# A local-attention and MLP kernel: a chunk's q, k and v fetched for all four head pairs by one set of transfers

## The chip, the cores and the metric

The kernel runs on one core of one Trainium2 chip. The time is the device time of one execution in microseconds (us), and runs are compared by their median. The names of the engines are those of the profile: PE is TensorE (matmuls), PEld its weight loads, DVE VectorE, ACT ScalarE, POOL GpSimd, SP SyncE, which here does nothing but issue DMA transfers. "SPq" is the queue of instructions on SP.

## The reference

There are 4 batches, 8 heads, 768 positions and a head dimension of 64. Attention sees the first `n_global` = 8 keys and, of the others, the last `n_local` = 96 positions up to the query, with a bias that falls linearly with the distance; its output goes through an MLP of width 512 to 2048 to 512.

```python
scores = matmul(q, k.T) / sqrt(64)
keep   = (pos_k < n_global) | ((rel >= 0) & (rel < n_local))       # rel = pos_q - pos_k
scores = where(keep, scores - slope[h] * dist, -1e9)
x      = softmax(scores) @ v                                       # heads side by side: (3072, 512)
out    = gelu(x @ w_in) @ w_out                                    # w_in 512 x 2048, w_out 2048 x 512
```

All values arrive in single precision except the weights, which arrive as 64-bit words and are decoded on the chip.

## The kernel before

**Chunks and pairs.** The 3072 positions are cut into 12 chunks of 256 (`CT`), three to a batch; `c` counts chunks, and a chunk with `c % 3 == 0` is the `first` of its batch and has fewer keys. The 8 heads go in 4 pairs (`p`), two heads of 64 on the 128 partitions. For each chunk and pair there is a sequence: `load` fetches q, k and v; `split` scales q on POOL (L167, one instruction for a pair); `scores_pair` (L312) makes the scores on PE and reduces them on DVE (L346); `exps` (L356) takes the exponentials on ACT (L363) and normalises on DVE for chunks 0 and 1, on POOL for the others (L372); `flip` transposes on PE (L382) and copies the result `pt` out of PSUM on ACT (L386); `av_pair` (L389) multiplies with v on PE (L412) and writes x as two parts, `xh` on ACT (L435) and the remainder `xl` on DVE (L436, which shows as the helper's line L173).

**The MLP.** The width 2048 is cut into 8 slices of 256 (`s`). `m1` (L449) makes a slice of the hidden layer from x, three products for each operand pair, since both sides are split in a high and a low part; `gelu` evaluates it twice on ACT (L459, L460) with the remainder on DVE; `m2` (L479) accumulates the output.

**The weights.** Each slice comes in 4 pieces of 512 KB (`load_words`, L178, names `w`). `split_weights` decodes a piece on ACT (L203) and DVE (L209, L211, L213), `part_weights` makes its high part on ACT (L223) and its low part on DVE. There are 4 buffers for pieces under way, so a later piece is issued only when an earlier one is decoded. Later the same words are fetched a second time and compared (`check_load`, `check_words`, names `c`).

**The order of work.** `run` walks through numbered steps T and emits, at each, what the tables say. `STEPS` holds the MLP's steps: chunks 0 and 1 go through the slices in turn, so that the weights are decoded while two chunks use them; from chunk 2 on, a chunk goes through its 8 slices alone. `DECODE` says at which step a piece is decoded. `START[c]` is the step from which chunk c's attention is counted, and `EVENTS[c]` gives for each of its operations the step (relative to that) of each pair: `EVF` for chunks 0 and 1, `EV2` for chunk 2, `EVS` for the rest. `after` adds an order between two instructions. Within what data and these orders require, a scheduler places the instructions of each engine; each engine then works strictly in its order, SP too.

**Loads.** Chunk 0 is fetched by `load_first` in whole-chunk buffers. For every other chunk `load(c, p)` issues the transfers of one pair, all on SP through the local helper `sync` (L279): 1 for q, 5 for k and 6 for v, 12 in all (8 in a first chunk), 48 for a chunk. Each pair has its own buffers out of a pool of four sets:

```python
self.nat = pool("nat", 4)
kr = pool.tile([P, KW + 96 if cc == 0 else 2 * KW], F32, name=f"kr{c}_{p}", tag="kn", padded_shape=[P, 2 * KW])
qr = pool.tile([P, CT], F32, name=f"qr{c}_{p}", tag="qn")
vr = pool.tile([P, 4, 2, 64], F32, name=f"vr{c}_{p}", tag="vn")
```

so that pair p of a chunk can be fetched when pair p of the chunk before has been used up. In `run`, chunk 1's four loads stand between the 4 pieces of the first weight slice and those of the others:

```python
for i in range(4):
    self.load_weights(0, i)
for p in range(NP):
    self.load(1, p)
for s in range(1, NST - 1):
    for i in range(4):
        self.load_weights(s, i)
```

Chunk 2's loads are ordered behind the last piece of the third slice, `word_ins[2, 3]`, and check pieces behind the loads of earlier steps.

Of the kernel before, what the change touches and what calls it, by code (L numbers as in the profile page):

```python
# [7 lines left out]
F32 = mybir.dt.float32  # L8
# [8 lines left out]
B, H, S, D = 4, 8, 768, 64  # L17
P = 128
# [15 lines left out]
MAXLOCAL = 97.0  # L34

START = [-7, -3, 7] + [8 * c - 7 for c in range(3, NCH)]
EVF = {"load": (-9, -9, -9, -9), "split": (-1, -1, -1, -1), "s": (0, 1, 2, 3), "pt": (2, 3, 4, 5), "av": (2, 3, 4, 5)}
EV2 = {"load": (-4, -3, -1, 1), "split": (-1, 1, 3, 5), "s": (0, 2, 4, 6), "pt": (1, 3, 5, 7), "av": (2, 4, 6, 8)}
EVS = {"load": (-4, -3, 0, 1), "split": (-2, -1, 2, 3), "s": (0, 0, 4, 4), "pt": (2, 3, 6, 7), "av": (4, 4, 8, 8)}
EVENTS = [EVF, EVF, EV2] + [EVS] * (NCH - 3)  # L40


# [40 lines left out]
class Fast:  # L83
    def __init__(self, tc, ctx, qT, kT, v, w, out, limits):
        self.tc, self.nc = tc, tc.nc
        self.qT, self.kT, self.v, self.w, self.out = qT, kT, v, w, out
        self.limits = limits
        pool = lambda name, bufs=1, **k: ctx.enter_context(tc.tile_pool(name=name, bufs=bufs, **k))
        self.ctx = ctx
        self.early = ExitStack()  # L90
        self.es = self.early.enter_context(tc.tile_pool(name="es", bufs=1, side="right"))
        self.const = pool("const")
        self.wts = pool("wts")
        self.stg = pool("stg", 3)
        self.nat = pool("nat", 4)
        self.pp = pool("pp", 6)
        self.ptp = pool("ptp", 2)
        self.xp = pool("xp", 3)
        self.gp = pool("gp", 2)
        self.sm = pool("sm", 2)  # L100
        self.words = ExitStack()
        self.ws = self.words.enter_context(tc.tile_pool(name="ws", bufs=4))
        self.ps_acc = pool("ps_acc", 2, space=PSUM)
        self.ps = pool("ps", 6, space=PSUM)
        self.win, self.wout = {}, {}
        self.kt, self.qt, self.vt, self.raw = {}, {}, {}, {}
# [134 lines left out]
    def load_first(self):  # L241

        nc = self.nc
        kr = self.es.tile([P, NP, KW + 96], F32, name="kr0")
        qr = self.es.tile([P, NP, CT], F32, name="qr0")
        vr = self.es.tile([P, 4, DM], F32, name="vr0")
        every = [[S, P], [P * S, NP]]
        nc.sync.dma_start(qr[:, 0], dap(self.qT, 0, [[S, P], [1, CT]]))
        nc.sync.dma_start(kr[:, 0, 0:CT], dap(self.kT, 0, [[S, P], [1, CT]]))
        nc.scalar.dma_start(qr[:, 1:NP], dap(self.qT, P * S, [[S, P], [P * S, NP - 1], [1, CT]]))  # L250
        nc.sync.dma_start(kr[:, :, CT:CT + 96], dap(self.kT, 0, every + [[1, 96]]))
        nc.sync.dma_start(kr[:, :, CT + 96:], dap(self.kT, 0, every + [[1, NG]]))
        nc.sync.dma_start(kr[:, 1:NP, 0:CT], dap(self.kT, P * S, [[S, P], [P * S, NP - 1], [1, CT]]))
        self.load_v(nc.scalar.dma_start, vr, 0, 0, DM)
        for p in range(NP):
            v = vr[:, :, p * P:(p + 1) * P].rearrange("q n (h d) -> q n h d", h=2)
            self.raw[0, p] = (kr[:, p], qr[:, p], v)

    def load_v(self, dma, vv, v0, cc, w):
        row = lambda r, n: dap(self.v, v0 + r * DM, [[DM, n], [1, w]])  # L260
        q0 = cc * CT
        if cc:
            dma(vv[0:NC, 0, :], row(q0 - 32, NC))
            dma(vv[NC:P, 0, :], row(0, NG))
        else:
            dma(vv[:, 0, :], row(0, P))
        dma(vv[0:NG, 1, :], row(0, NG))
        dma(vv[NG:P, 1, :], row(q0 + 96, NC))
        for j in range(2) if cc else (1,):
            o = HQ * j if cc else 0  # L270
            dma(vv[o:o + HQ, 2:4, :],
                dap(self.v, v0 + (q0 + j * P - 96) * DM, [[DM, HQ], [160 * DM, 2], [1, w]]))

    def load(self, c, p):
        nc = self.nc
        b, cc = divmod(c, CPB)

        def sync(out, in_):
            ins = nc.sync.dma_start(out, in_)  # L279
            if c == 2:  # L280
                self.after(ins.ins, self.word_ins[2, 3], "behind the first slices")
            return ins

        k0 = (b * H + 2 * p) * D * S
        v0 = b * S * DM + p * P
        pool = self.nat
        kr = pool.tile([P, KW + 96 if cc == 0 else 2 * KW], F32, name=f"kr{c}_{p}", tag="kn", padded_shape=[P, 2 * KW])
        qr = pool.tile([P, CT], F32, name=f"qr{c}_{p}", tag="qn")
        vr = pool.tile([P, 4, 2, 64], F32, name=f"vr{c}_{p}", tag="vn")
        self.last_load = sync(qr, dap(self.qT, k0 + cc * CT, [[S, P], [1, CT]])).ins  # L290
        if cc == 0:
            sync(kr[:, 0:CT], dap(self.kT, k0, [[S, P], [1, CT]]))
            sync(kr[:, CT:CT + 96], dap(self.kT, k0, [[S, P], [1, 96]]))
            sync(kr[:, CT + 96:], dap(self.kT, k0, [[S, P], [1, NG]]))
        else:
            q0 = k0 + cc * CT
            sync(pairs(kr, NG, 352, NX + NC), dap(self.kT, q0 - 96, [[S, P], [192, 2], [1, NX + NC]]))
            sync(kr[:, 224:288], dap(self.kT, q0 + HQ, [[S, P], [1, NX]]))
            sync(kr[:, KW:KW + NX], dap(self.kT, q0 + 32, [[S, P], [1, NX]]))
            for o in (0, 192):  # L300
                sync(pairs(kr, o, 352, NG), dap(self.kT, k0, [[S, P], [0, 2], [1, NG]]))
        self.load_v(sync, vr.rearrange("p n h d -> p n (h d)"), v0, cc, P)
        self.raw[c, p] = (kr, qr, vr)

    def split(self, c, p):
        kr, qr, vr = self.raw.pop((c, p))
        self.hi_pool(qr, qr, self.qsc[:, p:p + 1])
        self.kt[c, p], self.qt[c, p] = kr, qr
        for hh in range(2):
            self.vt[c, 2 * p + hh] = vr[:, :, hh, :]  # L310

    def scores_pair(self, c, p):  # L312

# [75 lines left out]
    def av_pair(self, c, p):  # L389
# [3 lines left out]
        if p == 0:  # L393
            self.x[c] = (self.xp.tile([P, NP, CT], F32R, name=f"xh{c}", tag="xh"),
                         self.xp.tile([P, NP, CT], F32R, name=f"xl{c}", tag="xl"))
        if EVENTS[c] is EVS:
            if p % 2 == 0:
                return
            ps = range(p - 1, p + 1)
        else:  # L400
            ps = range(p, p + 1)
# [3 lines left out]
            av = [avb[:, j] for j in range(2)]  # L405
        else:
            av = [self.bank([P, n, P], f"av{c}_{p}_{j}") for j in range(2)]
        heads = {(i, hh): (self.pt_t.pop((c, 2 * q + hh)), self.vt.pop((c, 2 * q + hh)))
                 for i, q in enumerate(ps) for hh in range(2)}

        def add(out, lhs, rhs, start, stop):
# [11 lines left out]
        for i in range(n):  # L423
            for a in range(2):
                for j in range(2):
                    if first and j == 0:
                        continue
                    ks = slice(0, HQ) if first else slice(j * HQ, (j + 1) * HQ)
                    for hh in range(2):
                        pt, vt = heads[i, hh]  # L430
                        qs = slice(a * HQ, (a + 1) * HQ)
                        add(av[j][hh * D:(hh + 1) * D, i, qs], vt[ks, 2 + a, :], pt[ks, 2, qs], False, True)
        for j in range(2):
            xh, xl = (x[:, ps.start:ps.stop, j * P:(j + 1) * P] for x in self.x[c])
            nc.scalar.copy(xh, av[j])  # L435
            self.lo_dve(xl, av[j], xh)  # L436
# [64 lines left out]

    def run(self, flag_i):
# [14 lines left out]
        for self.T in range(START[0] - 1, last):  # L517
# [234 lines left out]
```

## Time and profile before

| what | value |
|---|---|
| median of 3 runs | 723.93 us (720.51 to 725.51) |
| the profiled execution's own time | 724.53 us |
| its span, first to last instruction | 722.7 us |
| mean granted PE clock | 0.974 |
| PE busy | 682.6 us (94%), 5485 matmuls |
| ACT busy | 358.9 us (50%) |
| DVE busy | 285.4 us (39%) |
| POOL busy | 108.5 us (15%) |
| DMA | 71.29 MB in 87164 packets, 99 GB/s over the span |

The profile is of one execution. Its views group instructions by source line, list what each engine waited for and what released it, follow the chain of work that ended last back from the end, and show the instructions in order of time. An engine's idle time costs something only where the end hangs on it. A wait for several things is put down to the one that came last. In views, `out<-in` names the tiles that an instruction writes and reads, and an x with a number counts instructions in a row.

### The profile page before, as it was taken

To read this page: it belongs to the slowest core of one execution; us is meant where nothing else is said; L and a number is where in the kernel's file an instruction comes from. 1 tells how busy PE (TensorE), PEld (TensorE's weight loads), DVE (VectorE), ACT (ScalarE), POOL (GpSimd) and SP (SyncE) were. 2 spreads that over 40 slices of the span, in tenths; PEclk is the share of its full clock that TensorE was granted. 3 is DMA by queue.
4 is the path that set the end of the run, shared out by engine and by line. 5 is a ranking of instruction groups with operands and counts; after the bars stand their busy time and mean duration, and the time that the engine had idled before them with its cause. 6 is when DMAs were issued, how large, how long until landed. Compare 5 with 4: busy or idle time off the path is not lost.

```text
span 722.7 us, 14534 instructions
## 1 busy us (share of the span) xinstructions
PE 682.6 (94%) x5485; PEld 595.3 (82%) x5485; DVE 285.4 (39%) x987; ACT 358.9 (50%) x868; POOL 108.5 (15%) x232
## 2 busy tenths in 40 slices
PE   6757888999999999999999999999999999999996
PEld 4445767788888988998988988988988988988895
DVE  6837878852242243243242243243242243231110
ACT  3737557863554554554543554554543554552211
POOL 4100104320120220220220220220210220110000
PEclk7969998999999999999999999999999999999998
DMA  8441777331332432331432433331432431100000
GB/s 260 110 163 31 241 243 234 128 115 33 114 100 73 128 96 77 118 102 57 117 90 83 129 91 83 117 95 61 121 94 80 128 91 25 52 1 2 31 0 34
DMA packets 87164, 71.29 MB, mean 99 GB/s; under 512 B 38064, under 2 KB 75440, under 8 KB 87088
## 3 DMA queue, kind: packets, MB, share of 16 engines
q1 hardware_dynamic: 82640, 62.82, 30.2%
q10 hardware_dynamic: 4448, 7.48, 3.0%
q8 instruction: 46, 0.75, 0.4%
q14 instruction: 30, 0.25, 0.1%
HBM read 63.97 MB, written 6.29 MB: 97 GB/s over the span
## 4 chain that ended last, share of the span: by engine, by line
PE 83%; DMA 6%; ACT 3%; SPq 3%; DVE 2%; POOL 1%; issue 1%; ACTq 0%; POOLq 0%; DVEq 0%
PE h L449 35%; PE acc L479 35%; PE av L412 5%; PE s L337 5%; PE t L382 4%; DMA w<-w 3%; SPq L279 3%; DMA kr<-kT 2%; ACT n L363 1%; POOL n L372 1%; DVE wb L211 1%; DMA nn_w<-limits 1%; DVE wb L213 0%; ACT w L203 0%; ACT L363 0%
## 5 line engine op out<-in xcount | busy, mean ns | idle before, releaser
L449 PE MATMUL h<-xh,winh 128*128 128x256 f32 x768 | 221.0, 288 | 0.0
L449 PE MATMUL h<-xl,winh 128*128 128x256 f32 x768 | 217.6, 283 | 0.0
L449 PE MATMUL h<-xh,winl 128*128 128x256 f32 x768 | 217.2, 283 | 0.0
L173 DVE TENSOR_TENSOR gl<-gr,gh 128x512 fp32r<-128x512 f32 x96 | 67.2, 700 | 335.5 <-ACT gr L460 335.4
L479 PE MATMUL acc<-wouth,gh 128*128 128x512 f32 x384 | 157.9, 411 | 8.0 <-ACT gh L459 7.9
L479 PE MATMUL acc<-woutl,gh 128*128 128x512 f32 x384 | 151.2, 394 | 0.0
L449 PEld LDWEIGHTS h<-xh,winh 128*128 128x128 f32 x768 | 146.8, 191 | 5.2 <-issue 1.1
L449 PEld LDWEIGHTS h<-xl,winh 128*128 128x128 f32 x768 | 147.1, 192 | 4.2 <-issue 0.5
L479 PE MATMUL acc<-wouth,gl 128*128 128x512 f32 x384 | 149.8, 395 | 0.2 <-DVE gl L173 0.2
L449 PEld LDWEIGHTS h<-xh,winl 128*128 128x128 f32 x768 | 147.0, 191 | 0.1
L459 ACT ACTIVATE gh<-h 128x512 fp32r<-128x512 f32 x96 | 57.4, 598 | 173.4 <-PE h L449 172.2
L372 POOL TENSOR_SCALAR n<-n,su 128x192 f32<-128x192 f32 (+1 forms) x160 | 73.3, 479 | 351.5 <-ACT n L363 206.8
L386 ACT COPY pt<-t 128x384 f32<-128x384 f32 x96 | 45.8, 481 | 101.8 <-PE t L382 101.8
L479 PEld LDWEIGHTS acc<-wouth,gh 128*128 128x128 f32 x384 | 72.7, 189 | 27.1 <-ACT gh L459 8.5
L479 PEld LDWEIGHTS acc<-wouth,gl 128*128 128x128 f32 x384 | 72.5, 189 | 17.9 <-DVE gl L173 1.1
L479 PEld LDWEIGHTS acc<-woutl,gh 128*128 128x128 f32 x384 | 72.9, 190 | 12.5
L412 PE MATMUL av<-pt,vr 64*64 64x64 f32 (+1 forms) x1024 | 49.5, 251 | 15.5 <-ACT pt L386 15.2
L363 ACT ACTIVATE n<-n,mn 128x192 f32<-128x192 f32 (+1 forms) x144 | 62.3, 434 | 1.5 <-DVE mn L346 1.3
L412 PEld LDWEIGHTS av<-pt,vr 64*64 64x64 f32 (+1 forms) x1024 | 37.3, 137 | 29.5 <-ACT pt L386 18.2
L346 DVE CUSTOM_DVE_ANT_0 n<-s,pen 128x192 f32<-128x192 f32 (+1 forms) x192 | 55.2, 341 | 11.5 <-PE s L337 11.3
L167 POOL TENSOR_SCALAR qr<-qr,qsc 128x256 f32<-128x256 f32 x48 | 30.6, 637 | 184.6 <-DMA qr<-qT 173.7
L460 ACT ACTIVATE gr<-h 128x512 f32<-128x512 f32 x96 | 56.8, 592 | 0.0
(73 smaller groups left out, 562.8 us busy)
## 6 DMA issues: line engine op xcount, KB each, us to landing
w<-w SPq DMA_DIRECT2D x32, 512.0 KB, 5.1
c<-w SPq DMA_DIRECT2D x32, 512.0 KB, 3.5
out<-o ACTq DMA_DIRECT2D x24, 256.0 KB, 2.7
qr<-qT SPq DMA_DIRECT2D x45, 128.0 KB, 2.4
vr<-v SPq DMA_DIRECT2D x88, 64.0 KB, 2.3
kr<-kT SPq DMA_DIRECT2D x32, 160.0 KB, 2.8
kr<-kT SPq DMA_DIRECT2D x128, 32.0 KB, 2.2
vr<-v SPq DMA_DIRECT2D x76, 48.0 KB, 1.9
```

Source lines behind the costliest of these rows:

```text
L167: self.nc.gpsimd.tensor_scalar(out=out, in0=in_, scalar1=scale, scalar2=0.0, op0=ALU.mult, op1=ALU.add)
L173: return self.nc.vector.tensor_tensor(out=out, in0=in_, in1=hi.bitcast(F32), op=ALU.subtract)
L337: ins = nc.tensor.matmul(out, lhsT=lhs, rhs=rhs, start=True, stop=True).ins
L346: ins = nc.vector.tensor_tensor_reduce(out=nn[:, j * NK:j * NK + n], in0=sp[hh][:, j, 0:n], in1=pen, scale=-slope(2 * p + hh), scalar=3e38 ...
L363: self.table(nc.scalar.activation(out=nn, in_=nn, func=AF.Exp, bias=mn[:, i:i + 1], scale=-1.0, accum_out=su[:, i:i + 1]))
L372: ins = eng.tensor_scalar(out=nn, in0=nn, scalar1=su[:, i:i + 1], scalar2=0.0, op0=ALU.mult, op1=ALU.add)
L386: nc.scalar.copy(pt, tp)
L412: ins = nc.tensor.matmul(out, lhsT=lhs, rhs=rhs, start=start, stop=stop, skip_group_check=True).ins
L449: nc.tensor.matmul(hp[:, f, :], lhsT=w[:, d, f * P:(f + 1) * P], rhs=x[:, d, :], start=n == 0, stop=n == 3 * NP - 1)
L459: self.table(nc.scalar.activation(out=gh, in_=hp, func=AF.Gelu))
L460: self.table(nc.scalar.activation(out=gr, in_=hp, func=AF.Gelu))
L479: nc.tensor.matmul(acc, lhsT=g[:, f, ks], rhs=w[:, f, :], start=s == 0 and n == 0, stop=s == NST - 1 and n == 5)
```

## The change

`load(c)` now fetches q and k of a whole chunk, and `load_v(c)` its v, into buffers that hold all four pairs, with one set of transfers: 1 for q, 8 for k (two that had covered two places at once are four now) and 6 for v, 15 in all; 8 in a first chunk. The bytes are the same. There is one such buffer for each of q, k and v where there were four of a quarter of the size, so the memory is the same, and a chunk's q and k are fetched when the last scores of the chunk before are made, its v when the last product of the chunk before is. The tables now give one step for `load` and one for `loadv`.

Two smaller edits come with it. In `av_pair` all chunks but chunk 0 now multiply with v two pairs at a time, where before chunks 1 and 2 went pair by pair. And in the first chunk of a batch x is written for both halves of the queries by one copy and one subtraction where there were two of each.

```diff
-EVF = {"load": (-9, -9, -9, -9), "split": (-1, -1, -1, -1), ...
-EV2 = {"load": (-4, -3, -1, 1), "split": (-1, 1, 3, 5), ...
-EVS = {"load": (-4, -3, 0, 1), "split": (-2, -1, 2, 3), ...
+EVF = {"load": -9, "loadv": -9, "split": (-1, -1, -1, -1), ...
+EV2 = {"load": -4, "loadv": -3, "split": (-1, 1, 3, 5), ...
+EVS = {"load": -3, "loadv": 1, "split": (-2, -1, 2, 3), ...
...
-        self.nat = pool("nat", 4)
+        self.nat = pool("nat")
...
+    def load_v(self, c):
+        self.vr[c] = self.nat.tile([P, 4, DM], F32, name=f"vr{c}", tag="vn")
+        self.rows_v(self.sync_of(c), self.vr[c], *divmod(c, CPB))
+
+    def load(self, c):
+        sync = self.sync_of(c)
+        b, cc = divmod(c, CPB)
+        k0 = b * H * D * S
+        q0 = k0 + cc * CT
+        kr = self.nat.tile([P, NP, KW + 96 if cc == 0 else 2 * KW], F32, name=f"kr{c}", tag="kn",
+                           padded_shape=[P, NP, 2 * KW])
+        qr = self.nat.tile([P, NP, CT], F32, name=f"qr{c}", tag="qn")
+        every = [[S, P], [P * S, NP]]
+        sync(qr, dap(self.qT, q0, every + [[1, CT]]))
+        keys = lambda o, n, k: sync(kr[:, :, o:o + n], dap(self.kT, k, every + [[1, n]]))
...
-            sync(pairs(kr, NG, 352, NX + NC), dap(self.kT, q0 - 96, [[S, P], [192, 2], [1, NX + NC]]))
-            sync(kr[:, 224:288], dap(self.kT, q0 + HQ, [[S, P], [1, NX]]))
-            sync(kr[:, KW:KW + NX], dap(self.kT, q0 + 32, [[S, P], [1, NX]]))
-            for o in (0, 192):
-                sync(pairs(kr, o, 352, NG), dap(self.kT, k0, [[S, P], [0, 2], [1, NG]]))
-        self.load_v(sync, vr.rearrange("p n h d -> p n (h d)"), v0, cc, P)
-        self.raw[c, p] = (kr, qr, vr)
+            keys(NG, NX + NC, q0 - 96)
+            keys(224, NX, q0 + HQ)
+            keys(KW, NX, q0 + 32)
+            keys(KW + 96, NX + NC, q0 + 96)
+            for o in (0, 192, KW + NX, KW + 256):
+                keys(o, NG, k0)
+        self.raw[c] = (kr, qr)
...
     def split(self, c, p):
-        kr, qr, vr = self.raw.pop((c, p))
-        self.hi_pool(qr, qr, self.qsc[:, p:p + 1])
+        kr, qr = self.raw[c]
+        self.hi_pool(qr[:, p], qr[:, p], self.qsc[:, p:p + 1])
...
-        if EVENTS[c] is EVS:
+        if c:
             if p % 2 == 0:
                 return
             ps = range(p - 1, p + 1)
...
+        if first:
+            xh, xl = (x[:, ps.start:ps.stop].rearrange("d p (j q) -> d j p q", j=2) for x in self.x[c])
+            nc.scalar.copy(xh, avb)
+            self.lo_dve(xl, avb, xh)
+            return
         for j in range(2):
...
-        for p in range(NP):
-            self.load(1, p)
+        self.load(1)
+        self.load_v(1)
         for s in range(1, NST - 1):
...
             self.att(T, "load")
+            self.att(T, "loadv")
```

More of the change, by code (lines that the diff above doesn't have):

```diff
@@ L36 @@
 START = [-7, -3, 7] + [8 * c - 7 for c in range(3, NCH)]
-EVF = {"load": (-9, -9, -9, -9), "split": (-1, -1, -1, -1), "s": (0, 1, 2, 3), "pt": (2, 3, 4, 5), "av": (2, 3, 4, 5)}
-EV2 = {"load": (-4, -3, -1, 1), "split": (-1, 1, 3, 5), "s": (0, 2, 4, 6), "pt": (1, 3, 5, 7), "av": (2, 4, 6, 8)}
-EVS = {"load": (-4, -3, 0, 1), "split": (-2, -1, 2, 3), "s": (0, 0, 4, 4), "pt": (2, 3, 6, 7), "av": (4, 4, 8, 8)}
+EVF = {"load": -9, "loadv": -9, "split": (-1, -1, -1, -1), "s": (0, 1, 2, 3), "pt": (2, 3, 4, 5), "av": (2, 3, 4, 5)}
+EV2 = {"load": -4, "loadv": -3, "split": (-1, 1, 3, 5), "s": (0, 2, 4, 6), "pt": (1, 3, 5, 7), "av": (2, 4, 6, 8)}
+EVS = {"load": -3, "loadv": 1, "split": (-2, -1, 2, 3), "s": (0, 0, 4, 4), "pt": (2, 3, 6, 7), "av": (4, 4, 8, 8)}
 EVENTS = [EVF, EVF, EV2] + [EVS] * (NCH - 3)
@@ L105, in __init__ @@
         self.win, self.wout = {}, {}
-        self.kt, self.qt, self.vt, self.raw = {}, {}, {}, {}
+        self.kt, self.qt, self.vr, self.raw = {}, {}, {}, {}
         self.pt_n, self.pt_t, self.x = {}, {}, {}
@@ L253, in load_first, with rows_v @@
         nc.sync.dma_start(kr[:, 1:NP, 0:CT], dap(self.kT, P * S, [[S, P], [P * S, NP - 1], [1, CT]]))
-        self.load_v(nc.scalar.dma_start, vr, 0, 0, DM)
-        for p in range(NP):
[L256 to L260, printed above, removed]
+        self.vr[0] = vr
+        self.rows_v(nc.scalar.dma_start, vr, 0, 0)
+        self.raw[0] = (kr, qr)
+    def rows_v(self, dma, vv, b, cc):
+        row = lambda r, n: dap(self.v, (b * S + r) * DM, [[DM, n], [1, DM]])
         q0 = cc * CT
@@ L271, in load_v, with sync_of @@
             dma(vv[o:o + HQ, 2:4, :],
[L272 to L276, printed above, removed]
+                dap(self.v, (b * S + q0 + j * P - 96) * DM, [[DM, HQ], [160 * DM, 2], [1, DM]]))
+    def sync_of(self, c):
         def sync(out, in_):
-            ins = nc.sync.dma_start(out, in_)
+            ins = self.nc.sync.dma_start(out, in_)
             if c == 2:
                 self.after(ins.ins, self.word_ins[2, 3], "behind the first slices")
[L282 to L290, printed above, removed]
+            self.last_load = ins.ins
+        return sync
@@ L291, in load @@
         if cc == 0:
-            sync(kr[:, 0:CT], dap(self.kT, k0, [[S, P], [1, CT]]))
-            sync(kr[:, CT:CT + 96], dap(self.kT, k0, [[S, P], [1, 96]]))
-            sync(kr[:, CT + 96:], dap(self.kT, k0, [[S, P], [1, NG]]))
-        else:
-            q0 = k0 + cc * CT
-            sync(pairs(kr, NG, 352, NX + NC), dap(self.kT, q0 - 96, [[S, P], [192, 2], [1, NX + NC]]))
-            sync(kr[:, 224:288], dap(self.kT, q0 + HQ, [[S, P], [1, NX]]))
-            sync(kr[:, KW:KW + NX], dap(self.kT, q0 + 32, [[S, P], [1, NX]]))
-            for o in (0, 192):
-                sync(pairs(kr, o, 352, NG), dap(self.kT, k0, [[S, P], [0, 2], [1, NG]]))
@@ L302, in load @@
-        self.load_v(sync, vr.rearrange("p n h d -> p n (h d)"), v0, cc, P)
-        self.raw[c, p] = (kr, qr, vr)
-    def split(self, c, p):
-        kr, qr, vr = self.raw.pop((c, p))
-        self.hi_pool(qr, qr, self.qsc[:, p:p + 1])
-        self.kt[c, p], self.qt[c, p] = kr, qr
-        for hh in range(2):
-            self.vt[c, 2 * p + hh] = vr[:, :, hh, :]
+            keys(0, CT, k0)
+            keys(CT, 96, k0)
+            keys(CT + 96, NG, k0)
+        else:
+            keys(NG, NX + NC, q0 - 96)
[4 more added lines that the diff above has]
+                keys(o, NG, k0)
@@ L312, in scores_pair @@
+        self.raw[c] = (kr, qr)
+    def split(self, c, p):
+        kr, qr = self.raw[c]
+        self.hi_pool(qr[:, p], qr[:, p], self.qsc[:, p:p + 1])
+        self.kt[c, p], self.qt[c, p] = kr[:, p], qr[:, p]
     def scores_pair(self, c, p):
@@ L407, in av_pair @@
             av = [self.bank([P, n, P], f"av{c}_{p}_{j}") for j in range(2)]
-        heads = {(i, hh): (self.pt_t.pop((c, 2 * q + hh)), self.vt.pop((c, 2 * q + hh)))
+        heads = {(i, hh): (self.pt_t.pop((c, 2 * q + hh)), self.vr[c][:, :, (2 * q + hh) * D:(2 * q + hh + 1) * D])
                  for i, q in enumerate(ps) for hh in range(2)}
@@ L493, in att @@
                 continue
+            if what in ("load", "loadv"):
+                if r == ev[what]:
+                    (self.load if what == "load" else self.load_v)(c)
+                continue
             for p in range(NP):
@@ L498, in att @@
                     else:
-                        {"load": self.load, "split": self.split, "s": self.scores_pair, "exp": self.exps,
+                        {"split": self.split, "s": self.scores_pair, "exp": self.exps,
                          "av": self.av_pair}[what](c, p)
@@ L510, in run @@
             self.load_weights(0, i)
-        for p in range(NP):
-            self.load(1, p)
+        self.load(1)
+        self.load_v(1)
         for s in range(1, NST - 1):
```

## The prediction

> **What bounds the kernel now.** First the waits of TensorE (PE), then the windows: start, length, busy time and instructions of PE, weight loads, VectorE (DVE), ScalarE (ACT), GpSimd (POOL), the granted PE clock, the DMA engines' busy share, GB/s.
>
> ```profile
> PE av L412 <- ACT pt L386: 15.2, 7, 8.6
> ...
> 36.80:44.90 8.10, 0.00 (x0) 0.00 (x0) 2.34 (x8) 1.97 (x7) 0.00 (x0) 0.69 0.68 232
> 153.00:722.00 569.00, 563.51 (x4595) 502.65 (x4586) 174.39 (x673) 265.14 (x642) 78.75 (x181) 1.00 0.28 80
> ...
> 44.90:53.70 8.80, 8.79 (x62) 6.89 (x62) 3.42 (x15) 3.04 (x7) 0.00 (x0) 0.51 0.33 116
> ```
>
> From 153 us on PE is busy 563.5 of 569 us, and what is left is about the tail behind the last matmul: nothing that only feeds PE can help there. What can be won lies before. The largest single wait is 8.6 us: from 36.8 to 44.9 PE does nothing at all, and in the 8.8 us behind it PE is busy throughout, at a clock of 0.51.
>
> Next the chain that ended last, cut to the first 80 us (start, length, what); then the timeline of the SP queue, ScalarE and PE (start, length, instruction, in brackets the idle time before it and what ended that).
>
> ```profile
> by line: SPq L279 24.8%; DMA kr<-kT 16.2%; DMA w<-w 10.3%; issue 5.4%; PE h L449 4.8%; DMA nn_w<-limits 4.6%; PE av L412 4.4%; PE s L337 4.2%; ACT n L363 4.2%; DVE wb L211 3.9%; ACT pt L386 2.0%; ACT wouth L223 2.0%; DVE wb L209 1.8%; DVE w
> 10.19 7.27 DMA kr<-kT
> ...
> 39.14 3.98 DMA w<-w
> ```
> ```profile
> 9.28 0.43 SPq L279 DMA_DIRECT2D qr<-qT  x1
> ...
> 35.86 3.16 SPq L279 DMA_DIRECT2D vr<-v  x6
> 39.14 33.01 SPq L178 DMA_DIRECT2D w<-w  x8
> ...
> 36.82 0.19 ACT L363 ACTIVATION_READ_ACCUMULATOR n<-n,nmax 128x1 f32 x1
> 43.14 0.67 ACT L203 ACTIVATE w<-w 128x512 int32<-128x512 uint32 x1 [6.13 <-DMA w<-w]
> ...
> 44.91 2.14 PE L412 MATMUL av<-pt,vr 128*64 128x128 f32 x24 [8.62 <-ACT pt L386]
> ```
>
> L279 is the helper `sync` in `load`: chunk 1's 48 transfers. They occupy the SP queue from 9.28 to 39.02 us, 29.7 us, and only behind them, at 39.14, is the first piece of the second weight slice issued. It lands at 43.1. ScalarE, which works in order, has been through with everything else since 37.01 and has stood 6.13 us at L203, that piece's decoding; the copy of `pt` on which PE waits is queued behind it. So PE's longest wait is named after ScalarE, but its root is the number of issues on SP.
>
> Are the bytes late, or the issues? The throughput of the DMA engines from 9 to 40 us, in 40 slices of 0.775 us:
>
> ```profile
> GB/s 386 412 315 214 285 412 418 412 392 345 215 53 70 89 95 211 208 87 78 37 32 71 81 94 186 244 84 52 79 48 72 106 177 248 86 65 77 36 66 93
> ```
>
> While the first weights flow it is near 412 GB/s, and from the twelfth slice (17.5 us) on mostly 50 to 100: the issues are late, not the bytes. The Trainium skill (DMA: Bandwidth & Descriptors, "Issuing engines are not separate DMA queues") says that the sequencer's time to start a DMA is usually small beside the DMA itself. By that rule the sum below would be zero; the trace differs, with 29.7 us of issuing for transfers that land 1.7 to 2.8 us after their issue (medians, below).
>
> **The change part by part.** *Fewer issues for chunk 1.* The row of an issue that already carries all four head pairs, and the sizes (KB each, us to landing):
>
> ```profile
> 2.13 0.51 SPq L252 DMA_DIRECT2D kr<-kT  x1
> ...
> qr<-qT SPq DMA_DIRECT2D x45, 128.0 KB, 2.4
> vr<-v SPq DMA_DIRECT2D x88, 64.0 KB, 2.3
> kr<-kT SPq DMA_DIRECT2D x32, 160.0 KB, 2.8
> kr<-kT SPq DMA_DIRECT2D x128, 32.0 KB, 2.2
> vr<-v SPq DMA_DIRECT2D x76, 48.0 KB, 1.9
> ...
> vr<-v SPq DMA_DIRECT2D x76, 16.0 KB, 1.7
> ...
> 20.00:30.00 10.00, 7.24 (x76) 4.41 (x75) 9.23 (x37) 6.44 (x21) 1.78 (x2) 1.00 0.48 117
> ...
> 25.12 0.97 PE L337 MATMUL s<-kr,qr 64*64 64x192 f32 x16
> ```
>
> The issue for all four pairs in the first row costs 0.51 us, no more than one for a single pair (29.7/48 = 0.62 with waits). 15 take 7.7 to 9.3 us, so SP is through between 17 and 19 us. From there the bytes count: per pair 128 KB of q, 160 + 4x32 = 288 of k, 2x64 + 2x48 + 2x16 = 256 of v, in all 4 x 672 KB = 2.75 MB, unchanged. At the rate of the 20 to 30 us window scaled to full share, 117/0.48 = 244 GB/s: at 19.3 us one pair's worth (0.69 MB) has moved before and after, but after it is q and k alone (1.70 MB); the missing 1.0 MB takes 4.1 us, to 23.4, and 2.4 us to landing make 25.8. v and the weight piece (1.57 MB) follow by 29.8, landing at some 32, ahead of 37.01, where ScalarE asks for it. The wait of 6.13 us goes: **-6.1**. Late next is `pt` itself, behind the remaining ScalarE work (44.91 - 43.14 = 1.8 us): PE starts at 38.8 and its gap shrinks from 8.6 to 2.5 us.
>
> *The clock behind the gap.*
>
> ```profile
> 78.81 0.50 PE L479 MATMUL acc<-wouth,gh 128*128 128x512 f32 x1 [3.01 <-ACT gh L459]
> ...
> 80.00:90.00 10.00, 10.00 (x68) 9.18 (x67) 6.99 (x14) 5.27 (x11) 1.12 (x1) 1.00 0.72 226
> ...
> 110.79 0.79 PE L479 MATMUL acc<-wouth,gh 128*128 128x512 f32 x1 [4.90 <-ACT gh L459]
> ...
> 110.00:116.00 6.00, 5.21 (x17) 3.89 (x17) 5.98 (x11) 4.36 (x9) 4.49 (x4) 0.59 0.65 211
> ```
>
> A gap of 3.01 us left the clock at 1.00; behind one of 4.90 it was 0.59 for 6 us. One of 2.5 should leave it. The 8.8 us stretch, where PE is the busy engine, shortens by 8.8 x (1 - 0.51): **-4.3** (0 if a gap over 3 us remains).
>
> *The set comes as a whole.* Pair 0's scores of chunk 1 start at 25.12 without a wait for data; by the 25.8 above they come **+0.7** late, and PE, in order, holds chunk 0's work behind them. Ends: 0, and +5.6 if k takes the 7.27 us to land that chunk 1's first k took behind the weights (chain above), 4.9 more.
>
> *Chunk 2's loads among the weight pieces.* These stand between pieces w on the same queue. The chain, 70 to 105 us, and the median landings:
>
> ```profile
> 71.81 4.27 DMA w<-w
> ...
> 81.11 5.99 DMA w<-w
> ...
> 90.39 3.85 DMA w<-w
> ...
> 100.49 4.46 DMA w<-w
> ...
> c<-w SPq DMA_DIRECT2D x32, 512.0 KB, 3.5
> ```
>
> Before, chunk 2's 48 issues are spread over steps 3, 4, 6 and 8; now q and k come at step 3, v at step 4. The last two hops (3.85 + 4.46 = 8.3 us) lose their competition: at 3.5 us, as the same 512 KB take in quieter times, **-1.3**. The first two get more; I take 0. Ends: PE's waits of 3.0 and 4.9 and the slow clock (6 x (1 - 0.59) = 2.5) all go, -10.4; or crowding, +8.0 (worked out under the rivals).
>
> *The rest.* One of chunk 0's copies of x:
>
> ```profile
> 20.94 0.25 ACT L435 CAST xh<-av 128x128 fp32r<-128x128 f32 x1
> ```
>
> Chunk 0's 8 become 4, as do those of chunks 1 and 2, with their subtractions. Chunk 0's would be done sooner, but PE's next wait is for `pt`, not for them; in the steady part PE, never out of work, hides them. 0; lower end -1, four times 0.25. Chunk 1 and 2's products with v go by twos; their x is complete at the same step. From chunk 3 on, q and k of the next chunk cannot be fetched before the last scores of this one, since there is one buffer: rows of a steady chunk follow with the rivals; 0.
>
> Sum: -6.1 - 4.3 + 0.7 - 1.3 = **-11.0 us**. The profiled execution took 724.53 us (span 722.7 and 1.8 around it), 0.6 over the median 723.93: 713.5, or **713** for a median.
>
> **The rivals.** *The weight waits go as well:* -6.1 - 4.3 + 0.7 - 10.4 = -20.1, 704. For it: 33 issues fewer stand between the pieces; against: 226 GB/s are moved there already (80 to 90 us). 0.22.
>
> *Crowding:* chunk 2's 2.75 MB instead of one pair's 0.69 stand ahead of the third slice's pieces: 2.06 MB at 226 GB/s are 9.1 us. The first of them was issued at 72.73 and decoded only at 80.64, some 3.6 us after it landed (4.27 behind its issue, as its neighbour), so 5.5 us reach PE, and a gap that long costs 2.5 us of clock: -6.1 - 4.3 + 0.7 + 8.0 = -1.7, 722. 0.10.
>
> Rows for this case (the timeline) and, from 339 us on, for the last of the rivals: a steady chunk in the timeline of PE and POOL, and a wait of the SP queue (in total, times, longest).
>
> ```profile
> 72.73 0.36 SPq L178 DMA_DIRECT2D w<-w  x1
> ...
> 80.64 0.70 ACT L203 ACTIVATE w<-w 128x512 int32<-128x512 uint32 x1
> ...
> 339.69 1.89 PE L337 MATMUL s<-kr,qr 64*128 64x128 f32 x24
> 344.09 1.54 POOL L372 TENSOR_SCALAR n<-n,su 128x128 f32<-128x128 f32 x4 [20.46 <-DVE su L366]
> 346.98 0.48 POOL L167 TENSOR_SCALAR qr<-qr,qsc 128x256 f32<-128x256 f32 x1 [1.35 <-DMA qr<-qT]
> 351.44 0.49 PE L382 MATMUL t<-ident,n 128*128 128x128 f32 x3
> SPq L178 <- DVE wand L237: 155.6, 18, 13.8
> ```
>
> *The set is late:* the upper end of that term, -6.1 - 4.3 + 5.6 - 1.3 = -6.1, 718. For it: k's many short rows now all precede v and the weights; against: SP no longer feeds them one by one. 0.06. The Trainium skill (Perfetto Trace Analysis, "DMA Optimizations") has this as a rule against such a change: splitting a transfer may let some of the work start sooner.
>
> *The issue time does not fall or hides nothing* (an issue for four pairs takes four times as long, or the queue stands until the bytes are through): 724. Against it stands the 0.51. 0.06. The Trainium skill's rule on the sequencer's time, above, comes to the same time.
>
> *Slower:* the single buffer. The q load waits for the scores that end at 341.6; if GpSimd's scaling of the next chunk's q stands ahead of this chunk's normalisation (344.09), that waits for the load, and PE's transposes at 351.44 for it. It decides from 7.8 us on (351.44 - 341.6 - 1.54 - 0.48 for the scaling). q alone takes 3.5 us, so SP would have to hold it behind a check piece that waits for VectorE, a mean 155.6/18 = 8.6 us: 12.1 - 7.8 = 4.3 us in each of 8 chunks, 34 us against -11: 747. Before, the check pieces stand behind the loads. 0.06.
>
> **How the numbers follow.** Forecast 0.50, the rivals in their order 0.22, 0.10, 0.06, 0.06, 0.06. The range runs from 702, the second case with a little of the copies, to 722, the crowded case; outside lie the last two rivals and thin edges of the first two. One per cent, 7.2 us, is about what a measurement of this kernel tells from no change. Faster by more (under 716.7): 0.47 of the forecast's 0.50, 0.22 of the second case's, 0.02 of crowding and 0.01 of the late set: 0.72. Slower: 0.06. Within: 0.22.
>
> **What would show it.** Right: on SP, 15 issues for chunk 1 and the next w before 25 us; no wait of ScalarE at L203 near 37; PE's longest wait under 5 us; the clock near 1 between 37 and 50. Wrong: chunk 1's scores waiting for kr past 27 us; L203 waiting longer than before between 70 and 90; any PE wait behind 153 us.

## The result and the profile after

| what | before | after |
|---|---|---|
| median, runs on the same chip | 724.72 us (720.51 to 726.33, 4 runs) | 704.56 us (703.03 to 707.51, 4 runs) |
| profiled execution, its span | 724.53, 722.7 us | 707.51, 705.7 us |
| PE busy, PE idle (span less busy) | 682.6, 40.1 us | 682.2, 23.5 us |
| granted clock, median of all runs | 0.967 (34 runs) | 0.980 (4 runs) |

The ratio is 0.9735, with an interval from 0.9682 to 0.9789: 19 to 20 us less, nearly twice the forecast 11. Of the 17.0 us between the two spans, 16.6 are idle time of PE. The profiled execution is the longest of the four, and has the lowest clock of them (0.973; the others 0.979 to 0.982).

The page of the kernel after: its span, the busy row of PE, ACT and the others, the chain that ended last by engine, and the DMA packets (87164 before).

```profile
span 705.7 us, 13981 instructions
...
PE 682.2 (97%) x5485; PEld 597.9 (85%) x5485; DVE 281.1 (40%) x969; ACT 356.8 (51%) x850; POOL 103.5 (15%) x232
...
DMA packets 66040, 71.23 MB, mean 101 GB/s; under 512 B 32688, under 2 KB 49072, under 8 KB 65968
...
PE 85%; ACT 6%; DVE 4%; DMA 2%; POOL 1%; issue 1%; ACTq 0%
```

The chain of the first 80 us, by line. SP's issue time, a quarter of this chain before, is gone from its head.

```profile
by line: DMA w<-w 13.3%; ACT n L365 12.3%; PE h L456 8.1%; DVE n L374 6.4%; PE acc L486 4.7%; DMA nn_w<-limits 4.6%; PE s L339 4.2%; DVE wb L211 4.1%; issue 3.9%; DVE n L348 3.3%; DVE wb L213 3.2%; DVE wb L209 2.6%; DVE xl L173 2.5%; ACT gh
```

The timeline of SP, PE and ACT after, in order of time:

```profile
9.07 0.43 SPq L275 DMA_DIRECT2D qr<-qT  x1
9.99 9.75 SPq L275 DMA_DIRECT2D kr<-kT  x8
19.78 4.16 SPq L275 DMA_DIRECT2D vr<-v  x6
24.05 33.84 SPq L178 DMA_DIRECT2D w<-w  x8
26.65 1.56 PE L339 MATMUL s<-kr,qr 64*64 64x192 f32 x16
37.44 0.66 ACT L203 ACTIVATE w<-w 128x512 int32<-128x512 uint32 x1
42.96 0.60 ACT L466 ACTIVATE gh<-h 128x512 fp32r<-128x512 f32 x1 [1.76 <-PE h L456]
43.49 0.89 PE L414 MATMUL av<-pt,vr 128*64 128x128 f32 x10
44.30 0.88 PE L339 MATMUL s<-kr,qr 64*64 64x192 f32 x16
48.56 0.45 ACT L365 ACTIVATE n<-n,nmax 128x192 f32<-128x192 f32 x1
48.71 1.27 PE L414 MATMUL av<-pt,vr 128*64 128x128 f32 x38 [0.58 <-ACT pt L388]
64.01 0.60 ACT L466 ACTIVATE gh<-h 128x512 fp32r<-128x512 f32 x1
```

There are 15 issues for chunk 1 (1, 8 and 6: of the five for k three had covered two places each, and are six now), and behind them the first piece of the second slice leaves at 24.05 instead of 39.14. ACT decodes it at 37.44, with no idle time in front, where it had stood 6.13 us. The first GELU (L466, `gelu`) starts at 42.96; before it started at 52.98.

PE's waits (in total, times, longest), and three stretches in the columns of the prediction's windows:

```profile
PE acc L486 <- ACT gh L466: 5.5, 3, 2.3
PE t L384 <- DVE n L374: 3.3, 2, 1.8
```
```profile
20.00:29.50 9.50, 9.50 (x62) 5.61 (x63) 8.52 (x35) 5.83 (x20) 0.00 (x0) 0.50 0.90 243
40.00:43.00 3.00, 3.00 (x16) 3.00 (x16) 2.16 (x10) 1.24 (x2) 0.00 (x0) 0.52 0.28 61
153.00:700.00 547.00, 546.58 (x4459) 488.66 (x4457) 167.54 (x649) 254.60 (x614) 75.79 (x176) 1.00 0.27 81
```

The wait of 8.6 us is gone, no wait is over 2.3 us, and from 153 us on PE misses 0.4 us in 547. So whatever the change brought, it brought before 153 us, as foreseen.

### The profile page after: what moved, and what is told of

Read it like the earlier page. It is cut to its first block, busy times and chain, and to the rows that moved or that the text cites. A ratio compares the mean times of both kernels' runs of the same rounds, so it can differ in the third digit from the quotient of the medians.

```text
span 705.7 us, 13981 instructions
## 1 busy us (share of the span) xinstructions
PE 682.2 (97%) x5485; PEld 597.9 (85%) x5485; DVE 281.1 (40%) x969; ACT 356.8 (51%) x850; POOL 103.5 (15%) x232
## 2 busy tenths in 40 slices
DMA packets 66040, 71.23 MB, mean 101 GB/s; under 512 B 32688, under 2 KB 49072, under 8 KB 65968
## 3 DMA queue, kind: packets, MB, share of 16 engines
q1 hardware_dynamic: 61520, 62.80, 29.7%
## 4 chain that ended last, share of the span: by engine, by line
PE 85%; ACT 6%; DVE 4%; DMA 2%; POOL 1%; issue 1%; ACTq 0%
PE h L456 36%; PE acc L486 36%; PE av L414 5%; PE s L339 5%; PE t L384 4%; ACT n L365 2%; DMA w<-w 2%; ACT w L203 1%; ACT L365 1%; DVE n L374 1%; POOL n L374 1%; ACT gh L466 1%; DVE wb L211 1%; ACT L466 1%; DMA nn_w<-limits 1%
## 5 line engine op out<-in xcount | busy, mean ns | idle before, releaser
L466 ACT ACTIVATE gh<-h 128x512 fp32r<-128x512 f32 x96 | 57.4, 598 | 173.5 <-PE h L456 171.0
L384 PE MATMUL t<-ident,n 128*128 128x128 f32 x288 | 51.4, 290 | 5.0 <-DVE n L374 3.3
L414 PE MATMUL av<-pt,vr 64*64 64x64 f32 (+1 forms) x1024 | 47.8, 251 | 0.6 <-ACT pt L388 0.6
L339 PE MATMUL s<-kr,qr 64*64 64x192 f32 (+1 forms) x704 | 44.8, 345 | 3.2 <-DMA kr<-kT 1.7
```

The lines of the kernel that those rows point to most:

```text
L339: ins = nc.tensor.matmul(out, lhsT=lhs, rhs=rhs, start=True, stop=True).ins
L384: nc.tensor.transpose(tp[:, i, :], nn[:, o:o + P], self.ident)
L414: ins = nc.tensor.matmul(out, lhsT=lhs, rhs=rhs, start=start, stop=stop, skip_group_check=True).ins
L466: self.table(nc.scalar.activation(out=gh, in_=hp, func=AF.Gelu))
```

## The experiments

Theory A is the prediction: the gain is chunk 1's issues (the stall, and the clock behind it). Theory B is the prediction's first rival: chunk 2's 33 fewer issues between the weight pieces bring the rest. Theory C came after the result: one of the two small edits, which the prediction put at zero, brings it. Ratios are to the kernel before on the same chip (medians 723.71 to 726.3), with a 95% interval. The clock is the median of the granted clock of the timed runs.

| kernel | median | ratio | interval | clock | PE idle, profiled | first, second GELU |
|---|---|---|---|---|---|---|
| before | 724.72 | 1 | | 0.967 | 40.1 | 52.98, 78.16 |
| after | 704.56 | 0.9735 | 0.9682 to 0.9789 | 0.980 | 23.5 | 42.96, 64.01 |
| E1 loads only | 713.27 | 0.9841 | 0.9792 to 0.9889 | 0.973 | 27.3 | 43.20, 67.93 |
| E2 small edits only | 712.49 | 0.9811 | 0.9785 to 0.9838 | 0.975 | 33.1 | 48.40, 69.99 |
| E3 all sets split | 709.37 | 0.9793 | 0.9757 to 0.9828 | 0.975 | 28.6 | 48.36, 69.59 |
| E4 chunk 1 split | 711.72 | 0.9832 | 0.9797 to 0.9866 | 0.976 | 27.1 | 47.68, 68.96 |
| E5 chunk 2 split | 703.9 | 0.9724 | 0.9683 to 0.9766 | 0.983 | 25.0 | 41.52, 62.51 |
| E6 piece first | 718.47 | 0.9886 | 0.9849 to 0.9924 | 0.969 | 29.4 | 46.34, 71.63 |
| E7 filler | 728.35 | 1.0048 | 1.0021 to 1.0075 | 0.969 | 34.9 | 51.18, 85.14 |
| E8 copies undone | 704.3 | 0.9699 | 0.9674 to 0.9723 | 0.977 | 26.6 | 43.48, 68.76 |
| E9 twos undone | 713.94 | 0.9841 | 0.9817 to 0.9865 | 0.970 | 27.2 | 43.33, 70.10 |
| E10 twos in chunk 2 only | 710.86 | 0.9782 | 0.975 to 0.9814 | 0.972 | 27.7 | 43.57, 70.61 |
| E11 GpSimd helps | 710.2 | 0.9771 | 0.9738 to 0.9804 | 0.979 | 26.3 | 43.66, 67.73 |
| E12 pairs, later | 709.18 | 0.979 | 0.9745 to 0.9835 | 0.973 | 24.8 | 42.37, 69.08 |

### The parts alone: E1 and E2

E1 is the kernel after with both small edits undone, E2 the kernel before with both of them:

```diff
 # E1, from the kernel after; E2 the reverse, from the kernel before
-        if c:
+        if EVENTS[c] is EVS:
...
-        if first:
-            xh, xl = (x[:, ps.start:ps.stop].rearrange("d p (j q) -> d j p q", j=2) for x in self.x[c])
-            nc.scalar.copy(xh, avb)
-            self.lo_dve(xl, avb, xh)
-            return
```

> The changed kernel with the two smaller edits undone: products with v pair by pair in chunks 1 and 2, x of a first chunk written in two copies. Theory (they count for nothing, 0 and at most 1 us in the prediction): within 2 us of 704.6. Rival (the order of PE in the first 60 us, with chunk 1's product no longer ahead of the hidden layer, gave 3 to 7 us of the gain): 708 to 712, first GELU 2 us or more later than 42.96.

> The kernel before with the two small edits alone, loads pair by pair as before. If the parts add up: -8 to -9 us, 714 to 716. If the products by twos take away by themselves the stall that chunk 1's issues cause (PE no longer stands at chunk 1's first product), the two parts overlap and it is 708 to 712, as with the split set of all chunks (709.4). If they are worth something only once the pieces come early: 720 to 724.

The loads alone are worth 0.0159 x 724 = 11.5 us by the ratio, 10.4 by the medians; the sum was 11.0. The timeline and a window of E1:

```profile
38.45 1.42 PE L414 MATMUL av<-pt,vr 128*64 128x128 f32 x24 [2.36 <-ACT pt L388]
43.20 0.60 ACT L461 ACTIVATE gh<-h 128x512 fp32r<-128x512 f32 x1 [1.57 <-PE h L451]
```
```profile
37.00:47.00 10.00, 8.49 (x73) 6.15 (x73) 6.03 (x23) 7.52 (x19) 0.00 (x0) 1.00 0.33 107
```

The product starts at 38.45 behind a gap of 2.36 us (38.8 and 2.5 were foreseen), the clock is 1.00 behind it, and the first GELU comes 9.8 us earlier, as -6.1, -4.3 and +0.7 make 9.7. The small edits alone are worth 13.7 us (0.0189), where the prediction had zero. E2's timeline still has ACT's stall at the piece (in brackets):

```profile
43.30 0.67 ACT L203 ACTIVATE w<-w 128x512 int32<-128x512 uint32 x1 [6.14 <-DMA w<-w]
48.40 0.60 ACT L464 ACTIVATE gh<-h 128x512 fp32r<-128x512 f32 x1 [0.96 <-PE h L454]
```

Together the parts would make 3.5% (1.59 and 1.89), and the whole change makes 2.65%: they overlap. The first GELU comes 9.8 us earlier in E1, 4.6 in E2, and 10.0 with both. E1's time lies above both cases foreseen for it (about 704.6, and 708 to 712), and E2's beside the case in which the two parts overlap (708 to 712).

### Which loads: E3, E4 and E5

The kernel after, buffers and all, with the sets issued pair by pair again for all chunks (E3), for chunk 1 (E4) or for chunk 2 (E5):

```diff
+        if c == 1:                      # E5: c == 2; E3: True
+            for p in range(NP):
+                kp, qp, kk = kr[:, p], qr[:, p], p * P * S
+                sync(qp, dap(self.qT, q0 + kk, [[S, P], [1, CT]]))
...
```

> The changed kernel with every chunk's set issued pair by pair again (48 transfers, 32 in a first chunk) into the same whole-chunk buffers, at the same steps, same bytes. Theory (the number of issues on SP is what counted): the first evaluation of GELU, at 52.98 us before and 42.96 after the change, comes at 50 us or later, ScalarE waits at L203 near 37 us again, and the time is 715 to 724. Rival (buffers, steps and the products by twos did it): the GELU stays within 2 us of 42.96 and the time within 3 us of 704.6.

> The changed kernel with chunk 1's set alone issued pair by pair. Theory (chunk 1's issues cost the stall, -6.1 and -4.3 of the sum; those of chunk 2 the rest): the first GELU is late as before (50 us or later), and the time lies about 10 us above the changed kernel, 713 to 716. Rival (chunk 2's issues, which stand between the weight pieces, did most): within 4 us of 704.6.

> The changed kernel with chunk 2's set alone issued pair by pair. Theory (the part of the gain beyond 10 us came from chunk 2's issues standing no longer between the weight pieces): the first GELU stays at 43 us, the time rises by 5 to 9 us, to 710 to 714. Rival (that part came from the products by twos, or from chunk 1's lead): within 2 us of 704.6.

E5 stands where the kernel after does: chunk 2's fewer issues are worth nothing. ACT's wait for pieces, from 44 to 150 us, is 4.6 us after and 8.2 in E5:

```profile
ACT w L203 <- DMA w<-w: 4.6, 6, 1.8
```
```profile
ACT w L203 <- DMA w<-w: 8.2, 7, 2.3
```

So chunk 2's issues do make a wait, but the end does not hang on it. The waits of PE that theory B names, for the GELU from 66 to 153 us, did shrink, in before, after and E5:

```profile
PE acc L479 <- ACT gh L459: 7.9, 2, 4.9
```
```profile
PE acc L486 <- ACT gh L466: 3.5, 2, 2.3
```
```profile
PE acc L506 <- ACT gh L486: 2.1, 1, 2.1
```

They shrink without chunk 2's fewer issues as well, so theory B's mechanism falls. E4 costs 7.2 us against the kernel after (711.72 - 704.56), E3 4.8 (its interval overlaps those of E4 and of the kernel after). Both had been expected to cost more (713 to 716, and 715 to 724), and in both the first GELU came earlier than the 50 us foreseen. Chunk 1's set is worth 5 to 7 us with the small edits in place, less than the 10.4 to 11.5 of the loads without them. The split also brings back the smaller packets (87163 in E3, 66040 in the kernel after), so these three runs do not tell the number of issues from the size of the packets; E6, below, bears on that.

### Which small edit: E8 and E9

E8 is the kernel after without the merged copies (the second block of E1's edit), E9 without the products by twos (the first).

> The changed kernel with the merged copies of x undone, the products by twos kept. Theory A (products by twos): 703 to 707, second GELU near 64 us. Theory B (merged copies): 711 to 714, second GELU near 68 us.

> The changed kernel with the products by twos undone (chunks 1 and 2 pair by pair again), the merged copies kept. With both small edits undone the time was 713.3. Theory A (the products by twos gave the 8.7 us between that and the changed kernel): 711 to 714, second GELU near 68 us as there. Theory B (the merged copies of x did): 703 to 706, second GELU near 64.

E8 keeps the whole gain; E9 loses 9.4 us by the medians and stands at E1's ratio. The merged copies are worth nothing; the products by twos are worth 7.7 us (0.9841 - 0.9735) to 10.3 (0.9841 - 0.9699). How, is seen in part in the rows of E1 (by pairs) against those of after, above (by twos):

```profile
48.45 0.83 ACT L388 COPY pt<-t 128x384 f32<-128x384 f32 x2
48.95 1.42 PE L414 MATMUL av<-pt,vr 128*64 128x128 f32 x24 [1.74 <-ACT pt L388]
50.19 1.24 PE L339 MATMUL s<-kr,qr 64*64 64x192 f32 x16
52.73 0.46 ACT L365 ACTIVATE n<-n,nmax 128x192 f32<-128x192 f32 x1
67.93 0.60 ACT L461 ACTIVATE gh<-h 128x512 fp32r<-128x512 f32 x1
```

In E1 chunk 1's product of pair 1 stands on PE ahead of the scores of pair 3. It waits 1.74 us for `pt`, and the scores behind it, which need nothing from it, start at 50.19; their exponentials start at 52.73. By twos the first ten instructions of the couple's product run at 43.49 without a wait, the same scores start at 44.30, and the part of the product that waits for `pt` stands behind them, at 48.71; the exponentials start at 48.56. PE's own work is the same in both; what changes is which instruction is at the head of its queue while ACT is late.

How these earlier scores shorten the whole is not shown. The second GELU moves from 67.93 in E1 to 64.01, and it was taken for the sign of the effect, but E8 breaks that: the scores of pair 3 come early there, the second GELU is as late as in E1 (near 64 was foreseen), and the time is that of the kernel after.

```profile
45.73 0.83 PE L339 MATMUL s<-kr,qr 64*64 64x192 f32 x14
68.76 0.60 ACT L461 ACTIVATE gh<-h 128x512 fp32r<-128x512 f32 x1
```

### In which chunk, and why: E10 and E12

E10 leaves chunk 1 pair by pair and chunk 2 by twos. E12 has the products of both pair by pair, with banks and copies of their own, but emitted at the steps where those by twos stand:

```diff
 # E10
-        if c:
+        if c > 1:
 # E12
-EVENTS = [EVF, EVF, EV2] + [EVS] * (NCH - 3)
+EVF1 = dict(EVF, av=(3, 3, 5, 5))
+EV21 = dict(EV2, av=(4, 4, 8, 8))
+EVENTS = [EVF, EVF1, EV21] + [EVS] * (NCH - 3)
...
-        prev = self.last_av if EVENTS[c] is not EVF else None
+        prev = self.last_av if c > 1 else None
...
-        if c:
+        if EVENTS[c] is EVS:
```

> The changed kernel with chunk 1's products with v pair by pair again, chunk 2's by twos. With both pair by pair it was 713.9, with both by twos 704.6. Theory (chunk 1's product of the second pair stood between its scores and those of the fourth, so the exponentials of pairs 2 and 3 came in two rounds instead of one): nearly all of the 9 us is chunk 1's, 710 to 714, second GELU at 67 to 70 us. Rival (chunk 2's, among the weight pieces): 704 to 707, second GELU near 64.

> The changed kernel with the products of chunks 1 and 2 pair by pair, each with banks and copies of its own, but emitted at the steps of the version by twos: both products of a couple at the later one's step. Theory (what counts is when PE is asked for the first product of a couple, not that two share banks and copies): 704 to 708, second GELU 64 to 66 us. Rival (the sharing counts: half the PSUM banks, copies and subtractions): 711 to 714, second GELU near 69.

E10 stands 0.0059 below E9, with intervals that just miss each other, and 0.0047 above the kernel after, with intervals that overlap: about half of the gain is chunk 1's and half chunk 2's, but the halves are not exact, and the expectation that nearly all is chunk 1's is not borne out. E12 is as near to the middle (0.9790 between 0.9841 and 0.9735), between its two expected ranges, and its interval overlaps those of the kernel after and of E9. Its trace shows that it did not do what it was meant for:

```profile
48.13 1.04 PE L416 MATMUL av<-pt,vr 128*64 128x128 f32 x22 [1.17 <-ACT pt L390]
48.99 0.83 PE L341 MATMUL s<-kr,qr 64*64 64x192 f32 x16
```

The second product of the couple still stands ahead of pair 3's scores and waits for `pt`. So E12 does not part the place of the product from the sharing of bank and copies. Its second GELU, at 69.08, is nearly as late as E9's; yet its first copy of chunk 0's output is at 163.08, with 163.00 after and 166.87 in E9. How the two divide is open.

### The clock: E6 and E7

E6 is the kernel before with one line moved: the first piece of the second slice is issued behind chunk 1's first pair. E7 is the kernel before with 44 more matmuls on PE, whose result nobody uses, meant for the gap (88 instructions in the trace):

```diff
 # E6
-        for p in range(NP):
+        self.load(1, 0)
+        self.load_weights(1, 0)
+        for p in range(1, NP):
             self.load(1, p)
         for s in range(1, NST - 1):
             for i in range(4):
-                self.load_weights(s, i)
+                if (s, i) != (1, 0):
+                    self.load_weights(s, i)
 # E7
+                ins = self.nc.tensor.matmul(out[:, j * P:(j + 1) * P], lhsT=self.ident, rhs=self.ident, start=True, stop=True).ins
...
+            if T == -1:
+                self.fill()
```

> The kernel before with one transfer moved: the first piece of the second weight slice is issued behind chunk 1's first pair instead of behind all four; 48 issues as before. Theory (PE's 8.6 us wait is that piece's place in SP's queue): no wait of ScalarE at L203 near 37 us, first GELU at 43 to 45 us instead of 52.98, time 712 to 716. Rival (the issues or the late operands of pairs 1 to 3 hold chunk 1 up as well): the first GELU improves by less than 6 us and the time by less than 5.

> The kernel before with 44 filler matmuls (128 x 128, in nobody's result) on PE ahead of chunk 1's first product, where PE stood idle for 8.6 us; ScalarE's 6.1 us wait for the weight piece stays. Theory (the idle gap costs 4.3 us more because the clock behind it is halved): granted clock 1.0 from 45 to 54 us, first GELU 3 to 5 us earlier than 52.98, time 719 to 722. Rival (the halved clock hides nothing that the end waits for, or idle time is not what halves it): within 1.5 us of the kernel before, or slower by what the fillers push aside.

E6's timeline and window (the piece leaves at 21.16, behind 16 of the 48 issues):

```profile
21.16 0.36 SPq L178 DMA_DIRECT2D w<-w  x1
36.56 0.64 ACT L203 ACTIVATE w<-w 128x512 int32<-128x512 uint32 x1
38.29 2.12 PE L412 MATMUL av<-pt,vr 128*64 128x128 f32 x24 [2.35 <-ACT pt L386]
```
```profile
37.00:47.00 10.00, 8.71 (x60) 6.82 (x61) 5.29 (x21) 4.25 (x11) 0.00 (x0) 0.50 0.61 204
```

One issue moved takes 8.3 us (0.0114) off the kernel before: the stall was the place of that piece in SP's queue, which settles the root that the prediction named. It is less than was expected of it (712 to 716, and a first GELU at 43 to 45). Behind a gap of 2.35 us, as long as E1's 2.36, the clock is 0.50 where E1's is 1.00. The first GELU is 3.1 us later than E1's, and the ratios differ by 0.0045, 3.3 us (the intervals overlap). The order of PE's early work is the same in both, so the length of the gap alone does not decide the clock.

E7 did not test this. Its fillers in the timeline:

```profile
36.18 2.84 PE L360 MATMUL fill_ps<-ident 128*128 128x128 f32 x24
46.91 0.58 PE L458 MATMUL h<-xh,winh 128*128 128x256 f32 x1 [7.90 <-ACT xh L444]
50.98 6.86 PE L360 MATMUL fill_ps<-ident 128*128 128x128 f32 x60
```

Only the first 24 of 88 came before the gap, which stayed 7.90 us long, 4 came right behind it, and 60 stood in the way later (6.86 us). It shows what filler costs in the wrong place (1.0048), and nothing on the clock.

### A way past the result: E11

Pieces of the weights are decoded and parted on ACT and VectorE. In E11, made from the kernel after, every second low part goes to GpSimd:

```diff
-        self.behind(self.lo_dve(lo, af, hi))
+        if i % 2:
+            nc.gpsimd.tensor_tensor(out=lo, in0=af, in1=hi.bitcast(F32), op=ALU.subtract)
+        else:
+            self.behind(self.lo_dve(lo, af, hi))
```

> The changed kernel with the low part of every second weight piece (a subtraction of 128 x 512) made on GpSimd instead of VectorE, which is over 9 of 10 us busy from 50 to 70 and from 80 to 100 us. Theory (VectorE's decoding now sets the pace there): 16 x 0.6 us less on VectorE, 2 to 6 us faster, 699 to 703. Rival (the weight pieces' buffers or ScalarE set it, or GpSimd is slower and takes VectorE's time): 703 to 708.

It is 5.6 us slower than the kernel after by the medians (intervals overlap), and so beyond both cases foreseen. By group, in E11 and then in the kernel after (busy us, mean ns of one, idle before):

```profile
L228 POOL TENSOR_TENSOR winl<-wb,winh 128x512 fp32r<-128x512 f32 x6 | 11.3, 1880 | 28.8 <-ACT winh L223 28.8
L209 DVE TENSOR_SCALAR wb<-w 128x512 int32<-128x512 int32 x25 | 14.8, 597 | 3.0 <-DMA w<-w 1.6 <-POOL winl L228 1.2
```
```profile
L209 DVE TENSOR_SCALAR wb<-w 128x512 int32<-128x512 int32 x26 | 11.1, 430 | 1.9 <-DMA w<-w 1.9
```

GpSimd takes 1.88 us for one of these subtractions, and VectorE's first step of the decoding, which was not changed, goes from 430 to 597 ns. None of the kernels that were run is clearly faster than the kernel after: E5 and E8 are level with it.

## Why the prediction was right, and where not

**The stall, -6.1: right.** E1's product starts 0.35 us from the foreseen time; E6, which moves one issue, shows that the piece's place behind chunk 1's issues was the root, with the number and the packets of the transfers left as they were.

**The clock, -4.3: in E1 the clock came out as foreseen, but not for the reason given, and its worth is not shown alone.** The rule was read from two gaps of before (3.01 us at 1.00, 4.90 us at 0.59). E6 has a gap of 2.35 us and a clock of 0.50. The kernel after itself ran at 0.52 from 40 to 43 us, behind gaps of at most 1.09 us. E9, with E1's loads and its products pair by pair but another order on PE, also ran at 0.50 from 40 to 43 us, and its first GELU (43.33 against 43.20) and its ratio are close to E1's. In the median of the timed runs, (1 - clock) x span is 22.6 us in E6 and 19.2 in E1: the difference of 3.4 us repeats, and is that of their times (3.3). What puts the clock down in the one and not in the other is not settled; E7, meant for it, missed.

**The set comes later, +0.7: not seen.** Pair 0's scores start at 26.65 instead of 25.12, ahead of the 27 that would have shown the prediction wrong, but PE did not wait for data there. It was busy throughout from 20 to 29.50 us at a clock of 0.50 (window above), where the kernel before had 1.00. In E9, with the same loads and a clock of 1.00, they start earlier than before:

```profile
24.71 1.08 PE L339 MATMUL s<-kr,qr 64*64 64x192 f32 x16
```

In E6, with the loads pair by pair and a clock of 0.50 from 20 to 30 us, they start at 26.49. So the +1.5 goes with the clock, not with the set. The working behind the term was off in another place: SP was through at 23.9 us, not between 17 and 19. The eight transfers of k took 9.75 us to issue, 1.2 each against 0.43 for q. The row of 0.51 us from which they were costed is a transfer of 64 KB, while those of k have up to 320. The throughput of that time, in the same 40 slices from 9 to 40 us:

```profile
GB/s 393 410 299 233 359 418 423 423 367 387 365 322 299 317 221 174 308 143 190 82 346 270 217 349 296 386 69 37 106 285 254 37 0 0 0 53 190 386 48 21
```

It stays between 174 and 423 GB/s up to the seventeenth slice (22.2 us), where before it fell to 50 to 100 from 17.5 us on. That fits issues that now wait for bytes, where before the bytes waited for issues; the piece was still issued 13 us before ACT decoded it, and ACT did not wait.

**Chunk 2's loads, -1.3: not shown.** E5, with all 48 issues of chunk 2 back, is as fast. That is also why the first rival was not the cause, though its 704 is the time that came.

**"Chunk 1 and 2's products with v go by twos; their x is complete at the same step", 0: this is the step that failed.** It measured 7.7 to 10.3 us (E9 against the kernel after and E8), and the sentence is true and beside the point: it asks when x is complete, not what stands behind the first product on PE's queue. In front of the scores of the next pair a product that waits for ACT delays ACT's own next work, which is those scores' exponentials. E1's rows show this delay; that it makes up the whole of the 7.7 to 10.3 us is not shown. The merged copies, in the same paragraph of the prediction, were rightly zero (E8).

**The sum.** -11.0 was foreseen for all, and 10.4 to 11.5 us measured for the loads alone (E1). That the two agree so closely is in part luck: of its four terms the stall is shown, the clock came out for another reason, and the other two were not seen. With about 8 us for the twos that makes the 19 to 20 of the whole. The edits also change how much clock is lost: (1 - clock) x span is 23.8 us before, 14.4 after, 21.7 in E9, so between E9 and the kernel after 7.3 us go with the 7.7 of time. Time at a low clock costs only where PE is busy, and idle PE is itself seen ahead of low clocks, so the runs do not tell which of the two is cause here.

**The single buffer, crowding, and issue time that hides nothing** did not come. Behind 153 us PE misses 0.4 us (above). SP's 29.7 us of issuing are 14.9. ACT's waits for pieces from 66 to 110 us, before and after:

```profile
ACT w L203 <- DMA w<-w: 9.1, 6, 3.2
```
```profile
ACT w L203 <- DMA w<-w: 3.2, 3, 1.8
```

They are 5.9 us less, where crowding would have made them more. The rule of the Trainium skill (DMA: Bandwidth & Descriptors, "Issuing engines are not separate DMA queues"), by which issuing would have been too small to matter, does not hold here for 48 small transfers in a row: in E6 one place in the queue was worth 8.3 us.

## What to carry to other kernels

Where an engine's longest wait is named after another engine that works in order, look for what that engine's queue stood behind, and follow it to the queue that issues the transfer: one issue moved ahead was worth 8 us here, and 15 issues in the place of 48 about 11, or 5 to 7 with the other edits in place. When an edit moves an instruction on an in-order engine, cost it by what stands behind it on that queue and who feeds on that, not by when its own result is complete. Gains in the same stretch need not add up (1.6% and 1.9% made 2.65%), so try each part alone before a sum is believed.

## What the runs showed of the hardware that was not expected

In the kernel after PE is busy for all of the 9.50 us from 20 to 29.50 us and its clock is 0.50 throughout; in E9, with the same loads, the same stretch has 1.00 (columns as above):

```profile
20.00:29.50 9.50, 6.97 (x74) 4.35 (x73) 8.53 (x34) 5.84 (x18) 0.00 (x0) 1.00 0.82 224
```

The Trainium skill (TensorE: Matmul & The Clock Gate, "What's actually happening") says that about 3.4 us of sustained work release the clock, and that the window runs freely, so that the moment varies. The second part fits these rows; the first does not hold for the small matmuls of this stretch, whose busy time is partly modelled.

The first issue of q for all four pairs cost SP no more than the first one for a single pair (0.43 us in both), but the eight issues of k behind it, of 64 to 320 KB, took 1.2 us each on average and up to 2.65. That the issuing engine then waits for the transfers ahead would fit the throughput of that time; no run tests it.
